# A state-space layer beside a dense layer on one Trainium2 core: block 4's dense 1 wholly as seven-product groups, their weights prepared in block 3

## The chip, the cores and the metric

The kernel runs on one core of a Trainium2 chip (trn2). The metric is the device time of one execution in microseconds (us). Engines are named as in the profile: PE is TensorE (PEld its weight loads), DVE is VectorE, ACT is ScalarE, POOL is GpSimd, SP is SyncE; a small q behind a name is its instruction queue. Lines such as L972 are lines of the kernel before.

## The reference: what is computed

The input x has 2048 rows of 1024 values. Three things are added: x itself, a state-space layer on the normalised x, and a dense layer on the normalised x:

```python
x = A_x
xn = _layernorm(x, axis=-1)
return x + _A_ref(xn, ...) + _B_ref(xn, B_w1, B_b1, B_w2)

# _A_ref: Bu = xn @ B_bar (complex); h[t] = Lam_bar * h[t-1] + Bu[t]
#         y = 2 * real(h @ C) + xn * Dskip
# _B_ref: h = xn @ w1 + b1          w1 is 1024 x 3584
#         act = h * tanh(softplus(h))
#         out = act @ w2            w2 is 3584 x 1024
```

The matrices are bfloat16.

## The kernel before

**Blocks.** The rows are worked on in four blocks of 512 (`blk` 0 to 3 in the code, blocks 1 to 4 in the text). In each block the kernel forms dense 1 (x times w1, 28 weight tiles of 128 columns), the activation, the input projection of the state-space layer, its recurrence along the rows (`recur`, a scan on VectorE), and last an output stage (`tail`), in which dense 2 and the output projection add up in all eight PSUM banks. `finish` then adds a pair of banks to x on VectorE (L1281), and ScalarE's queue stores it. The next block can use a bank only after that.

**Dense 1 in two forms.** A plain tile (`first_tile`, L822) is eight matmuls of 128 x 128 weights against 512 columns of transposed x. In blocks 3 and 4 (`SPLIT`) only the first 12 tiles are plain. The other 16 go in four groups, w, x, y, z, of four tiles each. A group is a two by two block matrix times a two by two block matrix, done in the Strassen-Winograd manner: seven products (w1 to w7) take the place of eight, each of eight matmuls with 256 columns (`w_product`, L972). For that the weights are needed raw (products 1, 2, 4) and as sums and differences in float16 (products 5, 6, 3, 7), and x as four differences TT (`sums_x`, L1397, on GpSimd), one each for products 5, 6, 7 and 4. After each product ScalarE or VectorE evicts a bank (`w_evacuate`, L992, L995, L1009). The state-space layer's input projection is done in the same way with weights that stay on the chip (a to d, L901).

**How the groups' weights are made.** This happens once, in block 2's output stage, and goes through memory:

- `w_load`: GpSimd issues four loads of 256 KB of w1 a group, into places of `hb` and `act` whose earlier content must be used up;
- `w_abs` (L1063): ScalarE sums the absolute values of each row, two operations a group;
- `w_row_out`, `w_row_in`: the sums go out to memory and come back on all partitions (GpSimd's queue), so that
- `w_exponent` (L1087 to L1094): VectorE can take a maximum and form a power of two as the group's scale;
- `w_scale` (L1108): ScalarE scales the raw units; `w_sums` (L1125): VectorE forms the four sums and differences;
- `w_store` (L1098): GpSimd's queue stores each of the seven units (256 KB) into the memory tensor `wsd`. A later ring load reads two units at once.

**The ring.** All streamed weights go through seven slots of 512 KB, in one list (`items`), loaded by SyncE's queue in list order (L402). A load is issued when the slot seven items back is used up, and a load from `wsd` also waits until both of its units have been stored. The queue is in order, so a load that waits holds up all those behind it, and the transposes of x (L558) that stand in the same queue.

**The order.** Every engine works through its instructions in the order in which the Python code adds them. The strings `HEAD`, `WHOLE` and `PARTS` write the order of the products out by hand: a letter for the group, a digit for the product; r is the rotation ahead of the recurrence, g an activation chain on ScalarE (`chain`, L853), m its last product on VectorE (`chain_mul`, L859), u opens a bank of the output stage. In block 3's and 4's output stage the loop over j runs the recurrence. Ahead of it stands `next_stats` (L530 to L534, the statistics of the next block's rows, on ScalarE); at j = 5 `next_root`, `next_scale` (L538, L545) and the four transposes follow. `ln_skip` (L552, L554) adds xn times the skip vector to x on VectorE; the TT differences are written over xn, so each needs its `ln_skip` first. In blocks 3 and 4 both stand beside the plain tiles 1, 3, 5 and 7.

Of the kernel before, what the change touches and what calls it, by code (L numbers as in the profile page):

```python
# [163 lines left out]
def build_kernel(nc, A_x, A_Lambda_re, A_Lambda_im, A_B_re, A_B_im, A_C_re, A_C_im,  # L164
# [22 lines left out]
    PARTS = ("a2 a1 b2 b1 a5 b5 a6 b6 a3 b3 a7 b7 c2 d2 a4 b4 c5 c1 d5 d1 c6 c3 d6"  # L187
             " d3 c7 w1 d7 w5 w2 c4 d4 w6 r0 x1 x5 x2 w7 w3 r1 m0 x6 w4 y1 y5 y2 x7 x3 r2 m1 y6 x4"
             " z1 z5 g2 z2 y7 y3 z6 y4 u0 z7 u2 z3 u1 z4 u7 g3 r3 r4 r5 m2 r6 r7")
    NWQ = (NF - NPL) // 4  # L190
    W_SEQ = [("wxyz".index(o[0]), int(o[1])) for o in PARTS.split() if o[0] in "wxyz"]
    W_BANKS = ((3, 5, 7), (1, 5, 6), (4, 5, 7), (3, 5, 6))
    assert len(W_SEQ) == 7 * NWQ

# [103 lines left out]
    wsm = late("wsm", [P, 4, NWQ], f32, 192)  # L298
# [4 lines left out]
    wsd = nc.dram_tensor("wsd", [len(W_SEQ) // 2, P, 2048], bf16, kind="Internal").ap()  # L303
    b_wsd = [Buf("wsd%d" % i, parts=[Buf("wsd%d_%d" % (i, h)) for h in range(2)]) for i in range(len(W_SEQ) // 2)]
    wmd = nc.dram_tensor("wmd", [NWQ // 2, P, 2], f32, kind="Internal").ap()
    b_wmd = [Buf("wmd%d" % i) for i in range(NWQ // 2)]
    b_wmx = [Buf("wmx%d" % i) for i in range(NWQ // 2)]
# [70 lines left out]
    for blk in range(NB):  # L378
        n1 = NPL if blk in SPLIT else NF
        items += [("w1", g) for g in range(n1 // 2)] + [("ws", i) for i in range((NF - n1) // 4 * 7 // 2)]  # L380
        items += [("w2", g) for g in range(NF // 2)]
        items += [("c", j) for j in range(NJ)] if blk >= FAST else []
    n_loaded = [0]

    def ring_load():
# [11 lines left out]
        elif kind == "w2":  # L397
            dst = ring[:, s, :].rearrange("p (f d) -> p f d", f=2)
            src = B_w2[g * 256:(g + 1) * 256, :].rearrange("(f p) d -> p f d", p=P)
        else:  # L400
            dst, src = ring[:, s, :], (ctd if kind == "c" else wsd)[g]
        SP.dma(lambda e: e.dma_start(dst, src), s_ring[s],  # L402
               reads=[b_ctd[g]] if kind == "c" else [b_wsd[g]] if kind == "ws" else [], writes=[b_ring[s]])
# [543 lines left out]
    def w_out(i, ci):  # L947
        f0 = NPL + 4 * i + 2 * ci
        return f0, act[:, f0:f0 + 2, :], b_actf[f0:f0 + 2]

    w_pos = [0]

    def w_product(i, n):
# [3 lines left out]
        s, half = n_item[0] % NRING, w_pos[0] % 2  # L957
# [17 lines left out]
        w_pos[0] += 1  # L975
        if half:
            item_done()

    def w_evacuate(i, n, keep):
        X, Y, Z = W_BANKS[i]  # L980
        ig = wsm[:, 3, i:i + 1]
# [5 lines left out]
        def whole(dst, b_dst, b, ci, queue):  # L987
            f0 = NPL + 4 * i + 2 * ci
# [29 lines left out]
        if n == 6:  # L1018
            keep["w", i, "v"] = snap(X, 0, AC if i < 3 else VE)
# [4 lines left out]
        if n == 4:  # L1024
            f0, dst, b_dst = w_out(i, 1)
            whole(dst[:, :, 0:TH], b_dst, X, 1, AC if i < 2 else VE)
# [6 lines left out]
    W_RAW = (("h", 0), ("h", 8), ("a", 0), ("a", 8))  # L1033
    W_SUM = ((16, 18, 20), (22, 24, 26)) * 2
    held = []

    def w_sum_at(i):
        kind, t = w_raw(i, 1, 0)
        return [("a", t0) for t0 in W_SUM[i]] + [(kind, t)]

# [4 lines left out]
    def w_load(i):  # L1045
        sem = DmaSem(nc, "d_wraw%d" % i, nper=4)
        for ci in range(2):
            for kh in range(2):
                dst, b_dst = w_unit(w_raw(i, ci, kh))
                f0 = (NPL + 4 * i + 2 * ci) * P  # L1050
# [9 lines left out]
    def w_abs(i):  # L1060
        for ci in range(2):
            src, b_src = w_half(i, ci)
            aop(lambda e, src=src, ci=ci: e.activation(  # L1063
                CT[:, 0:4, 1, TB:D], src.rearrange("p (j t) -> p j t", j=4), AF.Abs, accum_out=wsm[:, ci, i:i + 1]),
                reads=b_src, writes=b_snap[0:2] + [b_wsm[ci][i]])

    def wmx(h):
        return snaps[:, 4 + h, D - TH:D]

    def w_row_out(h):  # L1070
        ii = slice(2 * h, 2 * h + 2)
        vop(lambda e: e.tensor_tensor(wsm[:, 0, ii], wsm[:, 0, ii], wsm[:, 1, ii], op=ALU.add),
            reads=b_wsm[0][ii] + b_wsm[1][ii], writes=b_wsm[0][ii])
        PO.dma(lambda e: e.dma_start(wmd[h], wsm[:, 0, ii]), DmaSem(nc, "d_wmd%d" % h),
               reads=b_wsm[0][ii], writes=[b_wmd[h]])

    def w_row_in(h):
        b_wmx[h].writer, b_wmx[h].readers = b_snap[2].writer, dict(b_snap[2].readers)
        PO.dma(lambda e: e.dma_start(wmx(h), wmd[h].rearrange("p j -> (p j)").partition_broadcast(P)),
               DmaSem(nc, "d_wmx%d" % h), reads=[b_wmd[h]], writes=[b_wmx[h]])  # L1080

    def w_exponent(h):
        ii = slice(2 * h, 2 * h + 2)
        m, g, ig = (wsm[:, n, ii] for n in (1, 2, 3))
        b_m, b_g, b_ig = (b_wsm[n][ii] for n in (1, 2, 3))
        gi, igi = g.bitcast(i32), ig.bitcast(i32)
        vop(lambda e: e.tensor_reduce(out=m, in_=wmx(h).rearrange("p (q j) -> p j q", j=2),  # L1087
# [8 lines left out]
    def w_store(i, n, t, b_t):  # L1096
        pos = W_SEQ.index((i, n))
# [7 lines left out]
    def w_scale(i):  # L1105
        for ci in range(2):
            t, b_t = w_half(i, ci)
            aop(lambda e, t=t: e.activation(t, t, AF.Copy, scale=wsm[:, 2, i:i + 1]),  # L1108
# [20 lines left out]
    def project_fast(order, open_unit):  # L1129
        keep = {}  # L1130
        split = order is PARTS
        w_pos[0] = 0
        for o in order.split():
# [11 lines left out]
            elif kind in "wxyz":  # L1145
                w_product("wxyz".index(kind), n)
                w_evacuate("wxyz".index(kind), n, keep)
# [260 lines left out]
    for blk in range(NB):  # L1408
# [37 lines left out]
        for f in range(NPL if blk in SPLIT else NF):  # L1446
# [3 lines left out]
        out_stage = tail(blk, n_item[0] + (len(W_SEQ) // 2 if blk in SPLIT else 0))  # L1450
        open_unit = next(out_stage)
        if blk in SPLIT:
            project_fast(PARTS, open_unit)
# [5 lines left out]
        if near:  # L1459
            for q in range(NQ):  # L1460
                next_stats(blk + 1, q)
        for j in range(NJ):
# [7 lines left out]
            if blk in SPLIT:  # L1470
                if j == 1:
                    chain_mul(3)
                    next(out_stage)
                if near and j == 5:
                    for q in range(NQ):
                        transpose_dma(q)
                continue
            if blk:
                if j == 0:
                    for i in range(2):  # L1480
                        w_load(i)
                    w_abs(0)
                if j == 1:
                    next(out_stage)
                    for i in range(2, NWQ):
                        w_load(i)
                    for i in range(1, NWQ):
# [17 lines left out]
            for i in {4: (0, 1, 2), 5: (3, 4, 5, 6), 6: (7, 8, 9, 10), 7: range(11, 16)}.get(j, ()):  # L1505
                rows_size(i)
        if blk + 1 < NB:
# [61 lines left out]
```

## Time and profile before

| what | value |
|---|---|
| three runs | 605.07 us median (604.8 to 606.01) |
| the profiled execution | 605.53 us; its span, first to last instruction: 604.3 us |
| granted TensorE clock | 1.00 |
| PE / DVE / ACT / POOL busy, share of the span | 99% / 84% / 65% / 21% |

Busy time by stretch (us from the span's start), from the answer for windows:

| stretch | what runs | PE | DVE | ACT | POOL |
|---|---|---|---|---|---|
| 384 to 428 | block 3: dense 2, recurrence | 44.00 | 42.71 | 29.81 | 0.00 |
| 428 to 456.5 | block 3: output projection | 28.50 | 12.93 | 4.34 | 0.00 |
| 456.5 to 477.3 | block 4: the 12 plain tiles | 20.80 | 14.82 | 12.67 | 9.93 |

The page gives averages over the span; a change in one stage is read from that stage's timeline. A group of instructions is shown with its line, engine, operation, what is written from what, the shapes and the number; what stands in square brackets is idle time before it and what ended it. Matmuls overlap, so their pace is read from the length of a piece of the chain divided by their number, not from the duration of one.

### The profile page before, as it was taken

The numbers are of one execution on the slowest core, as the hardware profiler recorded it, in microseconds if no ns is written. First come the engines' busy times: TensorE is split into PE (matmuls) and PEld (weight loads), VectorE is DVE, ScalarE is ACT, GpSimd is POOL, SyncE is SP. The second block draws the span as 40 slices with busy tenths as digits, with TensorE's granted clock in tenths as the row PEclk, the third lists the DMA queues.
The fourth block names the chain that finished last, engine by engine and source line by source line (L and its number), as shares of the span: only waits on it lengthen the run. The fifth ranks groups of instructions, "written<-read, shape, count | busy, mean of one in ns | idle before, by whom it ended". The sixth has DMA issues, their size and how long they took to land.

```text
span 604.3 us, 8914 instructions
## 1 busy us (share of the span) xinstructions
PE 599.9 (99%) x3439; PEld 333.2 (55%) x3439; DVE 504.7 (84%) x774; ACT 390.5 (65%) x360; POOL 124.2 (21%) x137
## 2 busy tenths in 40 slices
PE   8999999999999999999999999999999999999998
PEld 7644444444444486444444888544444688744444
DVE  6999999999997979969689679799917577789953
ACT  4589999379869897486566947993302955892000
POOL 2899300220114100431257300000004100000000
PEclk9999999999999999999999999999999999999999
DMA  9999995992695410699797728654756304854421
GB/s 249 263 260 302 232 175 175 284 293 85 182 329 204 143 68 1 225 325 284 212 362 298 261 73 286 202 172 140 193 173 227 139 2 163 290 174 151 163 71 69
DMA packets 103236, 119.36 MB, mean 198 GB/s; under 512 B 52890, under 2 KB 74010, under 8 KB 103194
## 3 DMA queue, kind: packets, MB, share of 16 engines
q1 hardware_dynamic: 93424, 91.05, 51.5%
q0 software_dynamic: 6080, 19.41, 9.7%
q10 hardware_dynamic: 3690, 8.34, 3.6%
q8 instruction: 27, 0.44, 0.3%
q14 instruction: 15, 0.12, 0.1%
HBM read 90.98 MB, written 15.73 MB: 177 GB/s over the span
## 4 chain that ended last, share of the span: by engine, by line
PE 65%; DVE 19%; ACT 12%; issue 2%; DMA 1%; POOL 1%; SPq 0%; ACTq 0%; DVEq 0%; POOLq 0%
PE ps L1213 38%; PE ps L901 12%; PE ps L972 8%; PE ps L822 7%; DVE hT L1178 3%; DVE hb L835 3%; ACT act L800 2%; ACT act L794 2%; ACT act L793 2%; DVE CT L774 2%; DVE CT L771 2%; DVE mt L1183 2%; DVE BT L1380 1%; DMA xx<-in_A_x_dram 1%; DVE SS L1391 1%
## 5 line engine op out<-in xcount | busy, mean ns | idle before, releaser
L1213 PE MATMUL ps<-ring,act 128*128 128x512 bf16 x896 | 195.3, 379 | 0.0
L1213 PEld LDWEIGHTS ps<-ring,act 128*128 128x128 bf16 x896 | 87.5, 98 | 103.6
L822 PE MATMUL ps<-xnT,ring 128*128 128x512 bf16 x584 | 126.7, 379 | 0.0
L822 PEld LDWEIGHTS ps<-xnT,ring 128*128 128x128 bf16 x584 | 56.9, 98 | 68.9 <-issue 0.3
L1213 PE MATMUL ps<-ring,hT 128*128 128x512 bf16 x378 | 82.1, 379 | 0.0
L1213 PEld LDWEIGHTS ps<-ring,hT 128*128 128x128 bf16 x378 | 36.9, 98 | 44.7
L1178 DVE TENSOR_TENSOR_SCAN hT<-cs,qi,hT 128x512 bf16<-128x512 f32 x48 | 58.9, 1269 | 0.0
L835 DVE TENSOR_SCALAR hb<-ps,par 128x512 bf16<-128x512 f32 (+1 forms) x59 | 39.4, 709 | 5.7 <-PE ps L822 5.3
L1183 DVE TENSOR_TENSOR mt<-hT,tab 128x1024 bf16<-128x1024 bf16 x64 | 41.4, 688 | 1.1
L992 ACT ACTIVATE snaps<-ps,par,wsm 128x256 f32<-128x256 f32 x44 | 23.9, 561 | 27.4 <-PE ps L972 26.6
L832 ACT ACTIVATE hb<-ps,par 128x512 bf16<-128x512 f32 x21 | 13.8, 690 | 42.7 <-PE ps L822 37.6
L1397 POOL TENSOR_TENSOR TT<-xnT 128x1024 f16<-128x1024 bf16 x6 | 14.6, 2432 | 127.1 <-DVE mt L552 127.1
L1281 DVE TENSOR_TENSOR xx<-ps,xx 128x1024 bf16<-128x1024 f32 (+1 forms) x16 | 18.6, 1188 | 21.5 <-PE ps L1213 21.4
L972 PE MATMUL ps<-TT,ring 128*128 128x256 f16 x256 | 32.2, 273 | 0.0
L867 DVE TENSOR_TENSOR mt<-hT,tab 128x1024 bf16<-128x1024 f16 x48 | 30.9, 686 | 0.4
L926 DVE TENSOR_TENSOR hT<-ps,snaps 128x512 f16<-128x512 f32 x36 | 24.6, 691 | 7.1 <-PE ps L901 4.1
L793 ACT ACTIVATE act<-hb 128x3584 bf16<-128x3584 bf16 x8 | 25.5, 3184 | 6.8 <-DVE hb L835 6.8
L853 ACT ACTIVATE hb<-hb 128x4096 bf16<-128x4096 bf16 x8 | 28.9, 3617 | 0.1
L1157 PE MATMUL ps<-xnT,BT 128*128 128x512 bf16 x128 | 27.8, 379 | 0.0
L1213 PE MATMUL ps<-CT,hT 128*128 128x512 bf16 x128 | 27.8, 379 | 0.0
L972 PEld LDWEIGHTS ps<-TT,ring 128*128 128x128 f16 (+1 forms) x256 | 25.0, 98 | 3.8
L1009 DVE SCALAR_TENSOR_TENSOR act<-ps,wsm,snaps 128x512 bf16<-128x512 f32 x24 | 17.8, 750 | 10.0 <-PE ps L972 8.8
(187 smaller groups left out, 971.6 us busy)
## 6 DMA issues: line engine op xcount, KB each, us to landing
ring<-in_B_w_dram SPq DMA_DIRECT2D x96, 512.0 KB, 4.4
ring<-wsd SPq DMA_DIRECT2D x28, 512.0 KB, 4.3
ring<-ctd SPq DMA_DIRECT2D x24, 512.0 KB, 3.5
wsd<-act POOLq DMA_DIRECT2D x20, 256.0 KB, 6.7
ctd<-act ACTq DMA_DIRECT2D x8, 512.0 KB, 4.2
out_dram<-xx ACTq DMA_DIRECT2D x15, 256.0 KB, 5.7
xx<-in_A_x_dram POOLq DMA_DIRECT2D x12, 256.0 KB, 7.0
act<-in_A_B_re_dram POOLq DMA_DIRECT2D x8, 256.0 KB, 4.9
```

The source lines that it names most:

```text
L793: aop(lambda e: e.activation(a, hs, AF.Exp), reads=[b_hb[g % 2]], writes=[b_act[g]])
L822: PE.mm(lambda e, k=k, w=w: e.matmul(ps[:, bank, :], lhsT=w, rhs=xnT[:, k, :], start=k == 0, stop=k == NK - 1), reads=[b_ring[s]] + b_xnT, ...
L835: vop(lambda e: e.tensor_scalar(hb[:, hs, ts], ps[:, bank, ts], b1(f), None, op0=ALU.add), reads=[b_ps[bank], b_par], writes=[b_hbf[hs]])
L853: aop(lambda e, src=src, fn=fn, bias=bias: e.activation(a, src, fn, bias=bias), reads=b_src, writes=b_a)
L867: vop(lambda e, s=s: e.tensor_tensor(mt[:, s, :, :], hT16[:, :, j, :], tab[:, s, j, :].unsqueeze(1).to_broadcast([P, 2, TB]), op=ALU.mult) ...
L901: PE.mm(lambda e, w=w, x=x, o=o, begin=begin, end=end: e.matmul(ps[:, bank, o:o + TH], lhsT=w, rhs=x, start=opens and begin, stop=end, ski ...
L926: vop(lambda e: e.tensor_tensor(dst, bank(b), src, op=ALU.add), reads=[b_ps[b], b_src], writes=b_hT[ci][j0:j0 + 2])
L972: PE.mm(lambda e, w=w, x=x, o=o, begin=begin, end=end: e.matmul(ps[:, bank, o:o + TH], lhsT=w, rhs=x, start=opens and begin, stop=end, ski ...
L1157: PE.mm(lambda e, j=j, ci=ci, k=k, bank=bank: e.matmul(ps[:, bank + ci, :], lhsT=BT[:, ci, j, k, :], rhs=xnT[:, k, :], start=k == 0, stop= ...
L1178: vop(lambda e, ci=ci, init=init: e.tensor_tensor_scan(out=hT[:, ci, j, :], data0=cj("r", j).to_broadcast([P, TB]), data1=hT[:, ci, j, :], ...
L1183: vop(lambda e, s=s: e.tensor_tensor(mt[:, s, :, :], hT[:, :, j, :], tab[:, s, j, :].unsqueeze(1).to_broadcast([P, 2, TB]), op=ALU.mult), ...
L1213: PE.mm(lambda e: e.matmul(ps[:, u, :], lhsT=lhsT, rhs=rhs, start=st_, stop=last), reads=reads, writes=[b_ps[u]], first=st_, last=last, te ...
```

## The change

In block 4 no tile of dense 1 is plain any more: three more groups, p, q and s (tiles 0 to 11), take their place, so there are seven groups and 49 products. Block 3 stays as it was, with the old 12 plain tiles and w to z. Block 4's order (`FULL`) begins with the products of the three groups interleaved; a few of the last ones stand among the projection's first:

```diff
+    PARTS = "a2 a1 b2 b1 a5 b5 a6 b6" + LATE
+    FULL = ("p1 p5 p2 q1 q5 p6 q2 s1 p7 s5 p3 q6 s2 p4 q7 q3 s6 q4 g0 a2 a1 s7 s3 b2 b1 s4 g1 a5 b5 a6 b6" + LATE)
+    QUADS = "pqswxyz"
...
+    W_BANKS = ((0, 2, 1), (3, 2, 4), (7, 2, 6), (3, 5, 7), (1, 5, 6), (4, 5, 7), (3, 5, 6))
```

`LATE` is the rest of the old `PARTS`. The banks of a group are X (products 1, 6, 7, 4), Y (2) and Z (5, 3). The 21 units of p, q and s stand ahead of the others in `wsd`, two to a ring item, the last alone (256 KB), so the ring loads for block 4 are these units in the order of `FULL`: p1 with p5, p2 with q1, q5 with p6, q2 with s1, p7 with s5, and so on. In the list they take the place of six loads of plain w1:

```diff
-        n1 = NPL if blk in SPLIT else NF
-        items += [("w1", g) for g in range(n1 // 2)] + [("ws", i) for i in range((NF - n1) // 4 * 7 // 2)]
+        n1 = 0 if blk == NB - 1 else NPL if blk in SPLIT else NF
+        items += [("w1", g) for g in range(n1 // 2)]
+        items += [("ws", i) for i in range(W_FIRST if n1 else 0, NU)] if blk in SPLIT else []
```

The weights of p, q and s are prepared in block 3's output stage (`near` is true there). The raw units of p lie in `hb` 0 to 7, those of q in `act` 0 to 7, those of s in `act` 8 to 15; the sums in `act` 16 to 27 and `hb` 8 to 13. `next_stats` moves from ahead of the recurrence to behind the first two groups' sums of absolute values:

```diff
-        if near:
+        if near and blk not in SPLIT:
             for q in range(NQ):
                 next_stats(blk + 1, q)
...
+                if near and j == 1:
...
+                    for i in range(NV):
+                        w_load(i)
+                    w_abs(0)
+                    w_abs(1)
+                    for q in range(NQ):
+                        next_stats(blk + 1, q)
+                    w_abs(2)
+                if near and j == 3:
+                    w_row_out(2)
                 if near and j == 5:
                     for q in range(NQ):
                         transpose_dma(q)
+                    w_row_out(3)
+                    w_row_in(2)
+                    w_row_in(3)
```

Row 2 holds the sums of p and q, row 3 that of s. Behind the recurrence, and ahead of the carry into the next block and of the four output additions, stands the rest, with block 4's skip additions and TT differences among it:

```diff
+        if blk == NB - 2:
+            w_exponent(2)
+            w_exponent(3)
+            w_scale(0)
+            for q in range(3):
+                ln_skip(blk + 1, q)
+            w_sums(0)
+            sums_x(0)
+            ln_skip(blk + 1, 3)
+            for i in range(1, NV):
+                w_scale(i)
+                sums_x(i)
+                w_sums(i)
+            sums_x(3)
         if blk + 1 < NB:
             carry()
```

Each of the seven stores of a group stands on GpSimd's queue where its `w_scale` or `w_sums` stands here. So that queue holds: three stores of p, four of p's sums, TT0, three of q, TT1, four of q's sums, three of s, TT2, four of s's sums, TT3. The products of p, q and s are evicted into `hb` 0 to 11 by the same operations as those of the other groups.

The small scale tensors get a second part for the three groups (`wsm_v`), over bytes that are used in block 1 only, and the helpers take a group's number in `pqswxyz`, so w to z become groups 3 to 6; nothing else is changed for these.

## The prediction, made before the changed kernel had run

> **What bounds the kernel now.** I read the page's chain of waits first, for the engine that sets the end.
>
> ```profile
> PE 65%; DVE 19%; ACT 12%; issue 2%; DMA 1%; POOL 1%; SPq 0%; ACTq 0%; DVEq 0%; POOLq 0%
> ```
>
> Over the whole span TensorE holds two thirds of the chain. That is an average, so I next read the same chain in order of time, around the places that are changed (start us, length us, what).
>
> ```profile
> 358.76 19.21 PE ps L972 x176
> ...
> 384.48 72.09 PE ps L1213 x334
> 456.57 20.72 PE ps L822 x96
> 477.29 21.83 PE ps L901 x200
> ```
>
> From 310.97 us to the end, blocks 3 and 4 are TensorE alone, each piece starting where the one before ends. A matmul that goes away there is time saved, and a TensorE wait that appears there is time lost in full. The 96 matmuls of L822 are the twelve plain dense tiles of block 4, which the change takes out.
>
> Then the timelines of VectorE and GpSimd, because the new preparation is theirs. VectorE at the end of block 3 and the start of block 4:
>
> ```profile
> 436.58 0.36 DVE L1197 TENSOR_TENSOR qi<-hT,cs 128x8 f32<-128x8 bf16 x2
> ...
> 448.84 1.23 DVE L1281 TENSOR_TENSOR xx<-ps,xx 128x1024 bf16<-128x1024 f32 x1 [11.34 <-PE ps L1213]
> ...
> 456.61 1.22 DVE L1281 TENSOR_TENSOR xx<-ps,xx 128x1024 bf16<-128x1024 f32 x1 [1.37 <-PE ps L1213]
> ...
> 459.14 2.61 DVE L552 TENSOR_TENSOR mt<-xn,dsk 128x1024 bf16<-128x1024 bf16 x1
> ```
>
> VectorE ends its recurrence at 436.6 and is free for only 11 us before the four output additions (L1281); until 436.6 it has no gap. GpSimd, at the same preparation one block earlier and at the TT differences of block 4:
>
> ```profile
> 302.78 1.60 POOL L1098 DMA_DIRECT2D wsd<-act  x3
> ...
> 458.61 2.60 POOL L1397 TENSOR_TENSOR TT<-xnT 128x1024 f16<-128x1024 bf16 x1 [121.21 <-DVE mt L552]
> ```
>
> A store of one unit (256 KB) costs GpSimd 0.53 us of issue, a TT difference 2.60. What follows a store, from the answer on line L1098 (all 28 stores) and from the page's DMA part (ring load, median):
>
> ```profile
> DMA to landing us min/median/max: 2.8/5.8/10.4
> ```
> ```profile
> ring<-wsd SPq DMA_DIRECT2D x28, 512.0 KB, 4.3
> ```
>
> **The gain.** The 96 matmuls of 512 columns take 20.72 us, 0.216 each. Three groups of seven products are 168 matmuls of 256 columns; the piece of 176 at L972 took 19.21 us, 0.1092 each (a product of eight: 0.873). So 168 x 0.1092 = 18.34 us, and the gain is **2.38 us**, if nothing waits. The pace of the new form isn't in doubt: the same instructions run in blocks 3 and 4 already.
>
> **What is added, and its cover.** Up to 428 us in block 3's output stage: 12 loads of w1 on GpSimd (0.75 each, L1052), idle there; 6 sums of absolute values on ScalarE (2.09 each with the accumulator read, L1063), where ScalarE has 14.2 us idle in 384 to 428; one short add each in two places on VectorE (0.15). The loads bring 3 MB beside TensorE's ring; in block 2's output stage the same lines bring 4 MB, and the chain there shows 340 matmuls in 73.38 us without a wait. I cost them at nothing on TensorE.
>
> On ScalarE the order is now: last chain ends 402.1; group p's loads can start when VectorE's product at 391.81 ends (394.1) and landed in 4.1 to 7.0 us in block 2, so p's two sums run 403.5 to 407.7; q's 408 to 412.2; then the statistics of block 4's x (10.1 us, 401.98 to 412.08 before) to 422.3; s's to 426.5; root with its table load (1.6) to 428.1. VectorE arrives at 427.5 and waits 0.6. So the scaling of xn and the four transposes are some 1.3 us later; the transposes were issued from 429.44 to 435.77 and x is first used at 456.57, so that is hidden. VectorE's recurrence ends at about 438.0.
>
> **What moves onto the path.** Block 4 now begins with ring units made in that same stage, and the order on each engine is fixed. I follow it to p7, the ninth product of block 4, which shares a ring unit with s5, the first sum of the last group.
> - VectorE, 438.0: exponents of p and q, seven small operations, 1.4 us (293.02 to 294.50) to 439.4. The exponent of s needs its row back: out at 429.1, 6.45 to the next issue (283.57 to 290.02), 0.54, landing 4.0 to 5.8: 440.5. With 1.4 it ends at 441.9.
> - Three skip additions (0.61 + 0.69 each): 445.8. Scaling of p on ScalarE (1.92 x 2, from 439.3) is done by then. Four differences of p at 0.69 (2.74 together at 298.20): 448.5. The last store of p is issued at **449.0**.
> - From there GpSimd's queue is full, in this order: TT0, three stores of q, TT1, four differences of q, three stores of s, TT2, then s5. That is 3 x 2.59 (median of twelve at L1397: 2.57 and 2.61) + 10 x 0.535 = 13.1: s5 is issued at **462.1**. VectorE has s5 ready before, about 457, with two waits of 2.0 counted in (L552 took 2.61 beside GpSimd's TT operation, 0.61 elsewhere), so GpSimd sets it.
> - Landing 5.8 (2.8 to 10.4): 467.9. SyncE's ring load of that unit waits for it; 4.3 (3.2 to 14.5, the long ones at 311 us among many stores): **472.2**.
>
> Without a wait p7 would start at 456.57 + 8 x 0.873 = 463.6. So the stall is 472.2 - 463.6 = **8.6 us**. Its bounds from the rows: 448.5 may be 446.0 (no wait for root or row), TT 2.12: 458.2 + 2.8 + 3.2 = 464.2, a stall of 0.6; at the other end 462.1 + 10.4 + 6.5 = 479.0, a stall of 15.4 (with 14.5 for the ring load, 23). I take the medians, since several stores are in flight, but fewer than at 311 us, because each step waits for the one before.
>
> The earlier waits lie inside this one. p1 needs bank 0, freed by the first L1281. VectorE reaches it after the other sums (2 x 2.74 + 1.3 behind 448.5), two waits of 2.0 and the carry (0.9): 460.2, so p1 starts near 461.4, not 456.6. p2 waits for q's first store, q5 for TT1, s1 for q's sums on GpSimd; each ends before 472. The output stores on ScalarE's queue hold up p1's eviction until the fourth L1281, near 465; also inside.
>
> After p7 each ring unit is eaten in 1.75 us, 300 GB/s, with nothing loaded ahead, where before seven units lay ready. The stretch 311 to 325 us moved 377 GB/s, so the ring can keep up, but not regain anything; I add **0.8** (0 to 3). ScalarE's first chain of block 4 starts 12 us later than at 469.4; its 23 us end some 1.4 us before w1's eviction needs ScalarE, 28 products after s6 and q4. Free, with little room.
>
> **Sum**: 8.6 + 0.8 - 2.38 = +7.0. The profiled execution took 605.53 (span 604.3 and 1.2 around it), so 612.5; the median of the three runs is 0.46 lower. I predict **612.0**.
>
> **Two rules against the trace.** The row: at 459.14 the product L552, which takes 0.61 elsewhere, took 2.61, and ended as GpSimd's 2.60 ended. The Trainium skill, SBUF — State Buffer, section "SBUF: two separate sides", calls the pair of ports that VectorE and GpSimd share an exclusive lock, held for the whole instruction. The row agrees; by that rule each of the four TT operations, now set among the sums, blocks VectorE once.
>
> No row here shows the granted clock below 1.00, and no TensorE gap in blocks 3 and 4. The Trainium skill, TensorE: Matmul & The Clock Gate, Part 1, says that an idle window of about 3.4 us halves the clock until a busy one has passed. By it, the 5 us gap before p1 would make the next products 1.75 us each; they wait for data anyway, so my estimate from that page is another 0 to 3 us.
>
> **The rivals.**
> - *Hidden* (chance 0.08, about 603): the units come in time, and the 2.38 stand. It decides at s5 landing by 463.6 - 4.3 = 459.3 with bank 0 free by 457. For it: in block 3 the same units never held up TensorE (L972 without a wait, 353 to 384), but there they had 40 us. Against: GpSimd alone needs 13.1 us after 449. Time: 605.1 - 2.4 = 602.7, up to 604.
> - *Banks only* (0.14): stores and loads at their shortest, so that only VectorE's lateness counts; p1 at 457.4 (no wait of 2.0) to 461.4, a stall of 0.8 to 4.8, net -1.6 to +2.4, and with part of the ring wait up to +3: 604 to 608.
> - *Crowded queues* (0.18): 21 stores, the ring and the output together want 8 MB in some 22 us, about the 377 GB/s seen; landings and loads go to the long ends, stall 13 to 23: 616 to 625.
> - The forecast has 0.60: 608 to 616.
>
> The range must leave out no more than 0.2: **605.0 to 621.0**. From the cases, with 0.2% (1.2 us; about what a measurement here can tell from no change) as the bound: faster 0.08 (hidden, and a little of the banks case), same 0.05, slower 0.87.
>
> **What would show it.** Right: the 96 matmuls gone, 168 more at the pace of 0.109, TensorE idle between 456 and 475 with DMA of ring<-wsd as releaser, the largest wait ahead of p7 or s1; GpSimd without a gap from 449 to 464; L1281 near 460. Wrong: TensorE without a gap at 456 (hidden), a wait that ends on VectorE (banks), or a wait in block 3 itself, before 456, which would mean that the added loads or the reordered statistics aren't covered.

## The result and the profile after

The changed kernel takes **620.88 us** (median of 6, 620.43 to 622.11); the kernel before took 605.13 beside it (6 runs, 604.8 to 606.01). The ratio is 1.026, 95% interval 1.0247 to 1.0273. Slower was right, +15.75 us instead of +7 was not, and the wait is not the one that was forecast. The profiled execution has a span of 619.2 us, 14.9 more than before's. Lines are from here on those of the changed kernel: L1232 is the output stage (L1213 before), L989 the groups' products, L1118 the stores, L573 the transposes, L1300 the output additions, L1416 the TT differences, L1145 the groups' sums, L417 the ring loads. In kernels with more lines they stand some lines further down (L993, L1306, L1424, and so on).

TensorE's timeline at the end of block 3 and the start of block 4 (start us, length us, what; in square brackets the idle time before it and what ended it):

```profile
428.40 19.16 PE L1232 MATMUL ps<-ring,hT 128*128 128x512 bf16 x86
448.84 8.79 PE L1232 MATMUL ps<-ring,hT 128*128 128x512 bf16 x39 [1.28 <-DMA ring<-ctd]
471.44 1.86 PE L989 MATMUL ps<-xnT,ring 128*128 128x256 bf16 x8 [13.81 <-DVE xx L1300]
```

There are two waits, and neither is p7's. Inside block 3, TensorE waits 1.28 us for c7, the last load of the output projection's weights (`ring<-ctd`). Then it waits 13.81 us ahead of the very first product, p1, until VectorE's first output addition frees bank 0. Behind p1 it waits for nothing more. The chain of waits in order of time:

```profile
471.30 0.01 DVE xx L1300
471.31 0.14 issue
471.44 18.09 PE ps L989 x144
```

These 144 matmuls take 18.09 us; at 0.1092 each they would take 15.72. The windows show why (stretch, its length, then busy time of PE, PEld, DVE, ACT, POOL, the granted TensorE clock, the DMA share, GB/s):

```profile
464.00:475.00 11.00, 3.56 (x17) 2.49 (x18) 10.59 (x11) 0.00 (x0) 5.91 (x6) 0.50 0.95 331
475.00:477.00 2.00, 2.00 (x17) 1.65 (x15) 0.64 (x1) 1.82 (x4) 0.00 (x0) 0.81 1.00 362
477.00:490.00 13.00, 13.00 (x120) 11.49 (x119) 4.62 (x7) 9.17 (x18) 0.00 (x0) 1.00 0.98 361
```

After the idle stretch the clock stands at half, and it is back at 1.00 from 477 us on. So the 14.9 us come apart as 1.06 (block 3 ends at 457.63 instead of 456.57) + 13.8 (bank) + 2.37 (clock) - 2.38 (the gain) = 14.85.

Why VectorE is late is seen in its own timeline. These are the lines that differ from what an instruction of that kind takes elsewhere, and the output additions:

```profile
439.52 0.42 DVE L1107 TENSOR_REDUCE wsm_v<-snaps 128x2 f32<-128x256 f32 x1 [2.56 <-DMA snaps<-wmd]
...
443.34 0.29 DVE L1107 TENSOR_REDUCE wsm_v<-snaps 128x1 f32<-128x128 f32 x1 [2.31 <-DMA snaps<-wmd]
...
452.54 2.84 DVE L569 TENSOR_TENSOR xx<-xx,mt 128x1024 bf16<-128x1024 bf16 x1
455.31 5.82 DVE L1145 TENSOR_TENSOR act<-act 128x1024 f16<-128x1024 bf16 x4
...
463.10 3.16 DVE L1145 TENSOR_TENSOR act<-act 128x1024 f16<-128x1024 bf16 x1
...
466.72 3.24 DVE L1218 TENSOR_TENSOR qi<-qi,qt 128x8 f32<-128x8 f32 x1
...
470.08 4.61 DVE L1300 TENSOR_TENSOR xx<-ps,xx 128x1024 bf16<-128x1024 f32 x4
```

Twice it waits for the rows of sums, 2.56 and 2.31 us. And four times an instruction, or a group of four, takes 2.1 to 3.1 us more than its like: 2.84 for 0.69, 5.82 for four of 0.69, 3.16 for 0.69, and 3.24 for 0.17, the small product in the carry. The excess is 2.15 + 3.06 + 2.47 + 3.07 = 10.75 us. GpSimd has exactly four TT differences of 2.13 there, each beside one of them. These are called port waits below, after the shared ports that the prediction names.

GpSimd's store chain went about as forecast in length, but from a later start. In its timeline the first line below ends with s's raw units; then comes TT2, and s5 is the first of the three stores behind it:

```profile
460.82 2.73 POOL L1118 DMA_DIRECT2D wsd<-act  x5 [0.18 <-issue]
463.57 2.13 POOL L1416 TENSOR_TENSOR TT<-xnT 128x1024 f16<-128x1024 bf16 x1
465.63 1.62 POOL L1118 DMA_DIRECT2D wsd<-hb  x3
```

So s5 is issued at 465.63 (forecast 462.1), because p's last store goes out at 452.13 instead of 449.0; from there the queue takes 13.5 us (forecast 13.1). s5 lands 4.9 us later (forecast 5.8). Its ring load is issued at 470.6 and lands 4.8 later (forecast 4.3), at 475.4 instead of 472.2. Block 3 ends at 457.63, and eight products of 0.873 later p7 would be due at 464.6; so alone this chain would have cost about 10.8 us (an estimate). It just isn't what ends last.

Last, SyncE's queue, first of the kernel before, then of the changed one:

```profile
429.44 6.33 SPq L558 DMA_TRANSPOSE xnT<-xn  x4
435.87 0.53 SPq L402 DMA_DIRECT2D ring<-ctd  x1
```
```profile
429.21 14.27 SPq L573 DMA_TRANSPOSE xnT<-xn  x4
443.57 0.53 SPq L417 DMA_DIRECT2D ring<-ctd  x1
```

The four transposes start at the same time, but hold the queue for 14.27 us instead of 6.33. The load of c7 behind them goes out at 443.57 instead of 435.87, and this is TensorE's wait of 1.28 us.

### The profile page after: what moved, and what is told of

It reads as the page before. It is cut to its first block, busy times and chain, and to the rows that moved or that the text cites. A ratio compares the mean times of both kernels' runs of the same rounds, so it can differ in the third digit from the quotient of the medians.

```text
span 619.2 us, 9168 instructions
## 1 busy us (share of the span) xinstructions
PE 597.4 (96%) x3467; PEld 342.1 (55%) x3511; DVE 524.0 (85%) x808; ACT 421.8 (68%) x393; POOL 143.9 (23%) x174
## 5 line engine op out<-in xcount | busy, mean ns | idle before, releaser
L1232 PE MATMUL ps<-ring,act 128*128 128x512 bf16 x876 | 193.8, 379 | 1.1
L1232 PEld LDWEIGHTS ps<-ring,act 128*128 128x128 bf16 x896 | 87.7, 98 | 103.4
L837 PE MATMUL ps<-xnT,ring 128*128 128x512 bf16 x477 | 105.1, 379 | 0.6
L1232 PE MATMUL ps<-ring,hT 128*128 128x512 bf16 x369 | 81.8, 379 | 1.8 <-DMA ring<-ctd 1.3
L837 PEld LDWEIGHTS ps<-xnT,ring 128*128 128x128 bf16 x488 | 47.8, 98 | 57.4
L1232 PEld LDWEIGHTS ps<-ring,hT 128*128 128x128 bf16 x378 | 36.9, 98 | 46.1 <-DVE mt L567 1.7
L989 PE MATMUL ps<-xnT,ring 128*128 128x256 bf16 x264 | 35.2, 279 | 13.8 <-DVE xx L1300 13.8
L989 PE MATMUL ps<-TT,ring 128*128 128x256 f16 x352 | 44.9, 276 | 0.0
L1008 ACT ACTIVATE snaps<-ps,par,wsm_w 128x256 f32<-128x256 f32 x44 | 24.0, 563 | 21.1 <-PE ps L989 20.3
L989 PEld LDWEIGHTS ps<-TT,ring 128*128 128x128 f16 (+1 forms) x352 | 34.8, 99 | 5.5 <-issue 0.2
L989 PEld LDWEIGHTS ps<-xnT,ring 128*128 128x128 bf16 (+1 forms) x264 | 26.4, 100 | 18.3 <-issue 14.3
L850 DVE TENSOR_SCALAR hb<-ps,par 128x512 bf16<-128x512 f32 (+1 forms) x54 | 35.7, 706 | 0.6 <-PE ps L837 0.2
L1068 POOL DMA_DIRECT2D hb<-in_B_w_dram x12 | 8.9, 753 | 108.7 <-DVE act L874 57.3
L1232 PE MATMUL ps<-CT,hT 128*128 128x512 bf16 x126 | 27.7, 379 | 0.1
L1008 ACT ACTIVATE snaps<-ps,par,wsm_v 128x256 f32<-128x256 f32 x18 | 9.7, 563 | 26.1 <-PE ps L989 25.8
```

What stands on the lines that cost most here:

```text
L837: PE.mm(lambda e, k=k, w=w: e.matmul(ps[:, bank, :], lhsT=w, rhs=xnT[:, k, :], start=k == 0, stop=k == NK - 1), reads=[b_ring[s]] + b_xnT, ...
L850: vop(lambda e: e.tensor_scalar(hb[:, hs, ts], ps[:, bank, ts], b1(f), None, op0=ALU.add), reads=[b_ps[bank], b_par], writes=[b_hbf[hs]])
L989: PE.mm(lambda e, w=w, x=x, o=o, begin=begin, end=end: e.matmul(ps[:, bank, o:o + TH], lhsT=w, rhs=x, start=opens and begin, stop=end, ski ...
L1008: aop(lambda e, o=o, p=p, j=j: e.activation(o, p, AF.Identity, scale=ig, bias=b1(f0 + j)), reads=[b_ps[b], b_par, b_ig], writes=b_dst)
L1232: PE.mm(lambda e: e.matmul(ps[:, u, :], lhsT=lhsT, rhs=rhs, start=st_, stop=last), reads=reads, writes=[b_ps[u]], first=st_, last=last, te ...
```

## The experiments

The theory behind the forecast: GpSimd's queue of stores makes the ring late. Against it, from the trace above: VectorE frees the banks late, by the port waits (a), the row waits (b) and the slow transposes (c). The ladder below takes them away one after the other. "Ring" means a wait for `ring<-wsd`, "banks" one for the output additions, "c7" one for `ring<-ctd`.

| run | median us (runs) | TensorE's waits from 425 us on | transposes, issue to landing, median / max us |
|---|---|---|---|
| before | 605.1 (6) | none | 4.1 / 4.8 |
| after | 620.9 (6) | banks 13.8, c7 1.3 | 8.1 / 13.0 |
| e5 gain alone | 602.9 (10) | ScalarE 0.2 | 3.7 / 4.5 |
| e3 rows early | 615.5 (1) | banks 10.1, ScalarE 0.8 | 6.8 / 9.1 |
| e4 banks first | 618.1 (1) | ring 11.1 | 8.7 / 9.6 |
| e6 banks between | 618.0 (1) | ring 9.3, c7 2.3 | 9.3 / 13.9 |
| e7 all on VectorE | 617.5 (4) | banks 9.4, others 3.4 | 13.4 / 22.2 |
| e8 TT on GpSimd | 616.1 (1) | ring 10.9 | 14.5 / 22.8 |
| e9 rows early, TT on VectorE | 609.8 (4) | ring 4.3, banks 1.4 | 6.6 / 9.3 |
| e10 transposes first | 606.7 (10) | ring 2.7 | 7.4 / 8.1 |
| e11 stores after | 611.0 (4) | ring 4.3 | 6.6 / 9.1 |
| e12 sums first | 613.0 (6) | c7 6.7, ScalarE 0.2 | 11.0 / 12.4 |
| e13 late output stores | 611.0 (6) | c7 3.7 | 9.6 / 11.2 |
| e14 c7 by ScalarE | 621.3 (5) | banks 14.2, others 2.0 | 20.9 / 24.5 |
| e15 apart | 609.9 (6) | ring 4.3 | 7.7 / 10.6 |
| e16 apart, c7 beside | 617.4 (4) | ring 8.8 | 15.5 / 17.1 |

The waits and transposes are those of one profiled execution each. The runs of e7, e10, e12 and e13 scatter by 6 to 9 us, so small differences between such rows say little.

**e5, the gain alone.** No preparation in block 3; the ring items of p, q and s read units of w to z instead, so the output is not the reference's.

```diff
+            if kind == "ws" and g < W_FIRST:
...
+                g = UNIT[like[raw[0], raw[1] and g < W_FIRST - 1]] // 2
...
-                    for i in range(NV):
-                        w_load(i)
...
+            for q in range(NQ):
                 ln_skip(blk + 1, q)
-            w_sums(0)
...
+                sums_x(q)
```

> Leaves out the preparation of p, q and s: block 4's 49 products run in the order of the changed kernel, but their ring units are units of w to z that block 2 has stored, and w's scale is used, so the output is not the reference's. The statistics stand where they stood before; the skip additions and TT differences of block 4 stay at the end of block 3. All theories: no wait at block 4's start, gain of 2.4 us over the kernel before, 602.7 us. If the seven-product form itself were part of the loss (evictions, scratch banks, GpSimd's TT operations), 604 or more.

Measured: 602.88, ratio 0.9972 (0.9958 to 0.9986). The gain of 2.38 is real (2.25 here); the loss comes with the preparation and the order that it brings. And the transposes land in 3.7 us when nothing of the preparation is in flight. In this kernel, too, three VectorE products take 2.61 us beside GpSimd's TT operations; they cost nothing, since VectorE still waits for TensorE ahead of its last two output additions.

**e3, rows early (b).** The rows' way out and back moves to j = 2 and j = 4, with the statistics between the groups:

```diff
+                if near and j == 2:
+                    w_row_out(2)
+                    w_row_in(2)
+                if near and j == 4:
+                    w_row_out(3)
+                    w_row_in(3)
                 if near and j == 5:
...
-                    w_row_out(3)
-                    w_row_in(2)
-                    w_row_in(3)
```

> The changed kernel with the two small row exchanges moved up: s's sums of absolute values ahead of the last two statistics, rows out at j = 2 and j = 4, each row read back right behind it. Theory banks: the 4.9 us that VectorE waits for the rows behind the recurrence go, the first output addition comes at 465.2; 615.5 to 616. Theory ring: the stores move up by the same 4.9, so the same time; this run tells the price of the rows and not the two theories apart.

Measured: 615.51. The exponents end at 439.58 instead of 444.55 and the output additions begin at 465.12 instead of 470.08: the 5 us arrive whole. With one broadcast of 64 KB beside them instead of 128 and 64 KB, the transposes hold SyncE for 10.1 us instead of 14.3, and the wait for c7 is gone. The port waits are unchanged, and so the banks still cost 10.05 us.

**e4 and e6, banks first.** The output stage stops after each group of rows, and the four output additions stand ahead of q's sums (three) and s's (one); the ring loads they set free are issued after the last store.

```diff
+            next(out_stage)
+            hold[0] = True
             w_exponent(2)
...
-                sums_x(i)
-                w_sums(i)
+            for q in range(3):
+                next(out_stage)
+            sums_x(1)
+            w_sums(1)
+            next(out_stage)
+            sums_x(2)
+            w_sums(2)
```

In e4 the first two lines stood the other way round, so that c7's load was held back too: it goes out at 455.73, behind the last matmuls of block 3 (455.65), which so used what lay in the slot before, and the first load of p's units goes out only at 456.16 (452.89 in e6). e6 is the same without that fault.

> The changed kernel with three of the four output additions ahead of q's sums, and the fourth ahead of s's sums, so that the banks come free early and the sums of q and s come later by 3.7 and 4.9 us; the same instructions in all. Theory banks: p1 starts near 458.5 instead of 471.4, and the time falls by 12: 608 to 610. Theory ring: p1 starts early, but TensorE then waits for q5, s1 and s5, whose stores come some 4 to 5 us later than in the changed kernel; p7 near 481 to 483 as against 480.6; time 620 to 623, with the gap of 13.8 split into several.

> As e4_banks_first, but only the ring loads from wsd are recorded later, not c's last one: three of the four output additions ahead of q's sums, the fourth ahead of s's. Theory banks: p1 near 457.5, time 608 to 610. Theory ring: TensorE waits in several places until p7 near 479 to 482; 618 to 621. Theory both (the two waits end within a few us of each other, so that freeing one leaves the other): p7 a little before the 480.6 of the changed kernel, 616 to 619.

Measured: 618.14 and 618.04. The waits of e6:

```profile
PE ps L993 <- DMA ring<-wsd: 9.3, 3, 5.3
PE ps L1236 <- DMA ring<-ctd: 2.3, 1, 2.3
```

p1 and p5 run at once, and then the ring is late by 9.3 us in all: 5.31 ahead of p2, 2.91 ahead of q5, 1.08 ahead of p7. The forecast had 8.6 + 0.8 = 9.4 for the ring, all at and behind p7. e6 moves q's and s's sums back, so its waits are not wholly those of the changed kernel. But a ring wait of about the forecast's size stood behind the one for the banks there too (the 10.8 us above against 13.8): both conditions held at once, and what ended last was the other one. Freeing the banks alone moved the time by less than 3 us (one execution each), and the loss from one releaser to the next.

**e9, TT on VectorE (a).** e3, and `sums_x(i)` on VectorE, nothing else:

```diff
-    def sums_x(n):
+    def sums_x(n, op=None):
...
-        pop(lambda e: e.tensor_tensor(TT[:, n, :, :], a, b, op=ALU.subtract),
+        (op or pop)(lambda e: e.tensor_tensor(TT[:, n, :, :], a, b, op=ALU.subtract),
...
-                sums_x(i)
+                sums_x(i, vop)
```

> The kernel with the early rows (615.5 us), and in it the four sums of two input blocks on VectorE instead of GpSimd; nothing else. In the run with the early rows four VectorE instructions that stood beside GpSimd's sums took 10.8 us longer than their like (2.84 for 0.69, 5.83 for 2.75, 3.16 for 0.69, 3.24 for 0.17). Theory of the shared access: these 10.8 us go and four times 0.69 are added, the first output addition begins at about 457 instead of 465.1, and the kernel takes 606 to 609 us. Rival, the ring: the banks come free at 458 but the stores and loads of the new tiles are not there; TensorE's wait becomes one for the ring at p1 or behind it, 611 to 615 us. If the long instructions had another cause than GpSimd they stay long, and the kernel takes 617 to 619 us.

Measured: 609.78, ratio 1.0076 (1.0059 to 1.0093), 5.7 us below e3. The same four places in VectorE's timeline:

```profile
447.59 0.69 DVE L569 TENSOR_TENSOR xx<-xx,mt 128x1024 bf16<-128x1024 bf16 x1
...
448.81 2.74 DVE L1145 TENSOR_TENSOR act<-act 128x1024 f16<-128x1024 bf16 x4
...
455.87 0.17 DVE L1218 TENSOR_TENSOR qi<-qi,qt 128x8 f32<-128x8 f32 x1
...
456.16 4.61 DVE L1300 TENSOR_TENSOR xx<-ps,xx 128x1024 bf16<-128x1024 f32 x4
```

All four excesses are gone, and the output additions begin 9.0 us earlier than in e3, though VectorE does four operations more. The banks still cost 1.37 us, and the ring now 4.3, which is between the two expectations. No wait is longer than 2.93 us, and the granted clock stays at 1.00 throughout.

**e7 and e8, all moved forward.** On top of e9: the scaling of p and q at j = 5 ahead of the transposes, c7's load between the second and the third, the output additions among the sums. e8 has the TT differences on GpSimd instead.

```diff
                 if near and j == 5:
+                    w_exponent(2)
+                    w_scale(0)
+                    w_scale(1)
+                    for q in range(2):
+                        transpose_dma(q)
+                    next(out_stage)
+                    for q in range(2, NQ):
+                        transpose_dma(q)
```

> All suspected waits taken away at once, with the same products and the same arithmetic: row exchanges early, the exponent and scaling of p and q already at j = 5, c's last ring load between the transposes, the TT differences on VectorE, the output additions among the sums. Theory both (row waits, port lock, bank release and the store chain together are the whole loss): from the rows, VectorE frees bank 0 by 451 and the last bank by 459, s5 is stored near 451 and in the ring by 462, ahead of p7 at 463.6; no wait on TensorE, 602.5 to 604. If DMA throughput (21 stores, ring, output) were a limit of its own: waits on the ring of 2 to 6 us stay, 605 to 609.

> As e7_all_vector with one thing changed back: the four TT differences on GpSimd. If the shared port costs VectorE 2.1 to 3.1 us for each of them, VectorE's last output addition comes some 6 us later than in e7 and GpSimd's stores behind TT0 later by 2.1: 604 to 609. If the cover is wide enough by now, the same time as e7.

Measured: 617.48 (613.5 to 619.2) and 616.07; a miss. VectorE in e7:

```profile
460.53 0.69 DVE L1424 TENSOR_TENSOR TT<-xnT 128x1024 f16<-128x1024 bf16 x1 [15.18 <-DMA xnT<-xn]
```

It stands 15 us before the first TT difference, for a transpose that took 22.2 us to land: (c), until now worth 1 us, is the largest of all. Neither theory had foreseen it, and e7 against e8 says nothing on the ports, since the transposes set both: in e8 TensorE waits 10.0 us for p1's ring load, because the stores of p's sums, in flight with the transposes, take over 18 us to land.

**e10, transposes first.** e7 with the four transposes together ahead of c7's load and of the scaling; behind the recurrence, p's sums stand one place later, behind the exponents and scaling of s, q's behind the first TT difference, and s's behind the second.

```diff
+                    for q in range(NQ):
+                        transpose_dma(q)
+                    next(out_stage)
                     w_exponent(2)
                     w_scale(0)
                     w_scale(1)
-                    for q in range(2):
-                        transpose_dma(q)
-                    next(out_stage)
-                    for q in range(2, NQ):
-                        transpose_dma(q)
```

> The run with everything on VectorE (617.5 us), with its four transposes of x all issued ahead of the load of c7 and of the first scaling of p; the first store stays at about 434 us. If the 15 us for which VectorE waited for the transposes came from their place behind the load and the stores, the last transpose lands before 445, VectorE waits for none, and the kernel takes 603 to 607 us. If it is the stores in flight that slow them, wherever they are issued, the third and fourth transposes still land ten or more us after their issue, and it takes 610 to 616 us.

Measured: 606.70 (604.7 to 610.6), ratio 1.0027 (1.0008 to 1.0046): 10.8 us below e7 by the order alone (all its moves together), and the nearest to the kernel before of all versions. The transposes land in 7.4 us though the stores begin at 434.6, and VectorE waits 1.50 us for them. What is left is the ring:

```profile
PE ps L993 <- DMA ring<-wsd: 2.7, 3, 1.3
```

**e11, stores after.** e10 with the scaling of p and q behind the recurrence, first store at 440.2. Two skip additions also move ahead of p's sums, the first output addition ahead of q's, and the second ahead of s's.

```diff
-                    w_exponent(2)
-                    w_scale(0)
-                    w_scale(1)
...
             hold[0] = True
+            w_exponent(2)
+            w_scale(0)
+            w_scale(1)
```

> The same with the scaling of p and q behind the recurrence, so that the first store is issued at about 440 us instead of 434, behind the transposes. If stores in flight slow the transposes, they land by 443 here, VectorE is done with the output additions at about 458 and the banks keep TensorE 2 us or less: 603 to 607 us, and this is faster than the run with the early stores. If the ring sets the end as in the run with the additions put between (waits of 9 us for the ring in all), it takes 610 to 614 us, whatever the transposes do, and the run with the early stores is the faster one.

Measured: 611.02 (1.0097, 1.0072 to 1.0123). VectorE waits for no transpose here, but p1 for the ring by 3.75 us, and then runs at a clock of 0.50 from 460 to 465. The rival held. p's sums are stored 5.6 us later than in e10, as the first store is, for they stand behind the raw stores of q and s on GpSimd's queue; that costs more than the transposes gain (6.6 us to land, 7.4 in e10).

**e12 and e13, the ring's remainder.** e12 puts p's sums, with their stores, ahead of the work for s, and q's ahead of the first TT difference; e13 is e12 with block 3's output stores (1 MB) moved to SyncE's queue behind the held loads.

```diff
             hold[0] = True
+            w_sums(0)
             w_exponent(3)
             w_scale(2)
-            w_sums(0)
             ln_skip(blk + 1, 0)
-            sums_x(0, vop)
             w_sums(1)
+            sums_x(0, vop)
```

> The run with the transposes first (606.7 us) had no wait for banks left, and three for the ring, 0.57, 0.91 and 1.25 us. In it the four stores of p's sums, whose data is there from 439.8 us on, stand behind raw stores of q and s on GpSimd's queue and are issued at 443.9 to 446.0. Here p's sums, and with them their stores, come ahead of the exponents and the scaling of s, and q's sums ahead of the first sum of input blocks; nothing else. If the place of these stores in the queue holds p1, they are issued from about 440 us, the wait at p1 goes and the others shrink: 604.5 to 606 us. If the DMA engines are simply full from 449 us on (they moved 400 to 420 GB/s there), the waits return at the next units: 606 to 607.5 us.

> The same, and the four stores of block 3's output rows (1 MB) moved from ScalarE's queue, where they are issued from 450 to 460 us, to SyncE's, behind the ring loads that were held back. If full DMA engines cause the remaining ring waits, these 1 MB are worth up to 2.5 us at 410 GB/s, and the kernel takes 603 to 605 us, at or a little below the kernel before (605.0). If only the order of stores and loads mattered, it takes what the run without this step takes, within 0.5 us.

Measured: 612.95 (611.4 to 620.3) and 610.99 (606.3 to 613.4); both missed. The ring's waits did go, all of them, in both. But c7 came late in their place (e12's waits):

```profile
PE ps L1236 <- DMA ring<-ctd: 6.7, 1, 6.7
```

The stores of p's sums, out from 440.85 us on (443.87 in e10), meet the last transposes; these hold SyncE's queue for 14.2 us (e10: 11.1), and c7's load stands behind them. That the stores' new place alone did it isn't certain: the row of s also came back 2 us later in this execution than in e10's.

**e14, c7 by ScalarE.** e13 with c7's load on ScalarE's queue, between the scaling of x and that of p.

```diff
+                    load_by[0] = AC
                     next(out_stage)
+                    load_by[0] = SP
```

> The run with the late output stores (611.0 us median, 606.3 to 613.4 in six runs) waited for one thing only: 3.69 us in its profiled execution for c7, whose load stands behind the four transposes on SyncE's queue (they held it for 12.6 us). Here ScalarE's queue issues the load of c7, between the scaling of x and that of p; nothing else. If the way of the stores over the transposes to c7 is what is left, TensorE waits for c7 no longer and the kernel takes 603 to 606 us, with the spread of its runs back under 2 us. Rival: the transposes go on being slowed by the stores, VectorE waits for them before the first sum of input blocks as it did (2.57 us), and the wait comes back as one for the banks at p1: 606 to 610 us.

Measured: 621.27 (620.4 to 622.8), no better than the changed kernel (620.88); the largest miss. The issues from 428 to 448 us (out from in, queue, operation, number, KB each, median us to landing):

```profile
ring<-ctd ACTq DMA_DIRECT2D x1, 512.0 KB, 16.3
xnT<-xn SPq DMA_TRANSPOSE x4, 20.9
```

c7's load, issued at 431.49 beside the transposes, makes them land in 20.9 us, and takes 16.3 itself (in e10, where it goes behind them, the loads of this kind have a median of 6.3). VectorE waits 14.26 us for them, and p1 11.9 for its bank.

**e15 and e16: what slows the transposes?** Both keep every store behind them, as e11 does, with the sums stored ahead of the next group's raw units and the output stores late. They differ in nothing but c7's load: SyncE's queue behind the transposes in e15, ScalarE's beside them in e16.

```python
            w_exponent(2)
            w_exponent(3)
            w_scale(0)
            ln_skip(blk + 1, 0)
            ln_skip(blk + 1, 1)
            w_sums(0)
            w_scale(1)
```

> The run with the stores behind the transposes (611.0 us) waited 3.75 us for p1's tiles, whose stores stood behind raw stores of q and s, and then paid about 1.5 us of low clock. Here the load of c7 and all stores still come behind the four transposes, but p's sums are stored ahead of q's raw tiles, q's sums ahead of s's, and block 3's output rows are stored behind the ring loads. If transposes and traffic kept apart is all it needs, no wait is left but the ring's in small pieces: 602.5 to 605.5 us, with a spread under 2 us. Rival: the later stores push the end of the chain past the need for p1 to p7, 606 to 610 us.

> The same, with c7's load issued by ScalarE's queue at about 431.5 us, beside the transposes, while no store is in flight before 440. If any 512 KB transfer beside them slows the transposes, they land 10 us or more after their issue (as in the run with c7 by ScalarE and early stores, 15.6 to 24.5), VectorE waits for them and the kernel takes 606 to 615 us. If it takes the stores to slow them, they land in about 7 us as in the run above, and the time is that of the run above within 1 us.

Measured: 609.89 (607.9 to 611.8) and 617.43 (615.0 to 618.5). The line of the transposes from 428 to 448 us, in e15 and in e16:

```profile
xnT<-xn SPq DMA_TRANSPOSE x4, 7.7
```
```profile
xnT<-xn SPq DMA_TRANSPOSE x4, 15.5
```

One plain load of 512 KB beside the transposes slows them, and it doesn't take the stores: the third transpose holds SyncE's queue for 5.27 us from 438.8 on (1.70 in e15), and the first store goes out at 443.4. The last transposes then meet stores as well; how much of the doubling is theirs can't be told. The row of s, in flight with them, lands in 13.6 us instead of 7.5, so the exponents and with them all stores are late. (e16's profiled execution also lost some 3 us in its first 100 us, before any changed line, waiting for ring loads of w1; how much of the 7.5 us between the medians is of that kind can't be told.) In e15 the ring's remainder is 4.3 us; the expected 602.5 to 605.5 was missed, its rival held.

No version that prepares these weights beats the kernel before.

## Why the prediction was right in sign and wrong in size

- **The gain** (2.38): right. e5 measured 2.25.
- **GpSimd's queue and the ring** (s5 at 462.1, in the ring at 472.2, a stall of 8.6 + 0.8): about right in size, a little early. s5 was issued at 465.63 and in the ring at 475.4, a stall of some 10.8 by the forecast's own reckoning; 3.1 of the 3.2 us are the later start (the row and the skip instructions of the next point), since the shorter landing and the longer queue and load nearly cancel. With the banks out of the way e6 shows 9.3 us of ring waits, but from p2 on rather than at p7, because p2 shares its ring unit with q1, q's first store.
- **"The earlier waits lie inside this one"**: this is the step that failed. The wait of p1 for its bank was 13.81 us, 3.0 more than the ring's chain alone would have cost. The forecast had VectorE at the output additions at 460.2; it came at 470.08, and so p1 at 471.44 against 472.2 for p7, eight products further on. The 9.9 us are: 6.75 for port waits (10.75 measured, "two waits of 2.0" counted, though the same text said that by the rule each of four TT operations blocks VectorE once), 2.65 for the second row (exponents at 444.55 against 441.9), and 0.46 between two skip instructions. e3 gave the row's share back, e9 the ports'.
- **"... the four transposes are some 1.3 us later; ... so that is hidden"**: wrong. They were not later at all (429.21), but 8 us slower, because the rows of sums came back beside them: 3.7 us to land with nothing of the preparation in flight (e5), 6.8 with a broadcast of 64 KB (e3), 8.1 with 128 and 64 KB (after). The forecast named the transposes' queue and did not name what stands behind them in it: c7's load. Price 1.06 us here. Where that load flies beside the transposes instead, it is more: e7 stands 10.8 us above e10, though other moves lie between them too, and e14 10.3 above e13, with nothing else changed.
- **The clock**, an estimate of 0 to 3 us outside the sum: 2.37. Now the rows show it: 0.50 behind the idle stretches of 13.8 us (after), 10.1 (e3) and 3.75 (e11), 0.58 from 460 to 463 behind 2.75 (e15), and still 1.00 behind 2.93 (e9). The Trainium skill, TensorE: Matmul & The Clock Gate, Part 1, puts the idle window at about 3.4 us; here the clock fell once behind less than that, so the two don't agree to the letter.
- **The rivals.** "Banks only" named the right place, with a cap of 4.8 us for a stall of 13.8: it took the same two port waits. "Crowded queues" held the time (616 to 625) for another reason. The range, 605 to 621, just held it, by the room left for crowded queues and not for what happened.

So the change loses because its preparation needs three things at once in 28 us: VectorE, SyncE's queue with the transposes, and the DMA engines, which have to move 21 stores of 256 KB and their loads besides the transposes. Taking one away shows the next: rows 5.4 us, ports 5.7, then order and ring. In e10, 3.8 us above e5, 2.7 are the ring's.

## What to carry to other kernels

Where several engines feed one start, follow each to its end and write down the latest arrival of each; a wait that "lies inside" another must be computed as carefully as the one it lies in. When an engine's work is moved into a busy stretch, count every neighbour of its shared port and every transfer of its queue, with what stands behind them, even those that were there before and cost nothing. A transfer that is due early and that everything waits for, like the transposes here, is better issued alone, not merely first in its queue.

## What the runs showed of the hardware

- **GpSimd's tensor operation beside VectorE.** In each of the four places an instruction of VectorE with two inputs in SBUF waited until GpSimd's operation had ended, whatever its own size: 128x8 float32 went from 0.17 to 3.24 us, 128x1024 from 0.69 to 2.84. Twice the cost is above 3.0, more than one TT operation (2.13); why isn't shown. With the TT operations on VectorE (e9) all four costs are gone.
- **Transposes by DMA beside other transfers.** The four are small packets: 4320 of the kernel before's packets from 422 to 445 us, with them, are under 512 bytes, and 132 from 400 to 428, without them. With only ring loads ahead of and behind them they land in 3.7 us; beside one broadcast of 64 KB in 6.8, beside that, a plain 512 KB load and late stores in 15.5, beside the load and early stores in 20.9. What flies with them is slowed too (16.3 us for 512 KB in e14, 18 for p's stores of 256 KB in e8). The Trainium skill, Advanced Engine Details and Errata, section "X-Bar Transpose (TRN2)", calls transpose DMAs as fast as regular ones. With little beside them that may pass, beside other transfers the runs here speak against it. Why they slow each other so much stays open.
- **Partition broadcasts.** A row of 1 KB spread over all partitions (128 KB) took 10.7 us to land beside the transposes in the changed kernel.
